# Mixer after a gated recurrence: later loads of U and V, w1 staged in activation buffers, second products in quarters, q and k products on VectorE

## Chip, cores and metric

The kernel runs on one core of one Trainium2 chip. The metric is the device time of one execution in microseconds (us); lower is better. Timed runs and the profiled execution are separate executions of the same program.

## What is computed

```python
f = 1 / (1 + exp(-f_logit))                       # attention, q k v f: (4, 8, 768, 48), float32
for t in range(768):
    state = f[:, :, t, :, None] * state + einsum('bhd,bhe->bhde', k[:, :, t], v[:, :, t])
    y[:, :, t] = einsum('bhd,bhde->bhe', q[:, :, t], state)
x = y.transpose(0, 2, 1, 3).reshape(4, 768, 384)  # then the mixer
u = x + (x.transpose(0, 2, 1) @ U @ V).transpose(0, 2, 1)   # U (768, 32), V (32, 768)
out = u + maximum(u @ w_ch1, 0) @ w_ch2           # w_ch1 (384, 1536), w_ch2 (1536, 384)
```

U, V, w_ch1 and w_ch2 arrive as 64-bit floats, everything else as 32-bit floats.

## The kernel before, in words

The work is cut into 16 **units**: a batch b (0 to 3) and a pair of heads; four units make a batch, and a batch's attention is followed by its **mixer**.

*A unit.* `prepare(n)` has five pieces: `gates` (the sigmoid of f, channels on partitions), `keep` (the scan X over time, L468), `keys` (kT = k times X), `read` (the scan Y, L485, called `read_back` by the loops) and `queries` (qT = q times Y, and the loads of unit n + 2). In batches 0 and 1 the inputs are turned by TensorE (L436) and the products read PSUM on VectorE (L448). In batches 2 and 3 VectorE turns them in blocks of 32 (L417), and the products run on GpSimd (POOL, L451). `attend(n)` has `kept` (kT turned on TensorE and copied to `kb`), `states` (`ds`, then the scan `st`, L560), `scores` (`sc`, masked to A on VectorE), `read` (`y` from the states) and `inner` (`y` from A, then the copy to x). So a unit is a chain that goes back and forth between TensorE, ScalarE and VectorE.

*A mixer.* `low_rank` (x with U), six `mix` (with V, added to x), six `turn`, then for each of three row pairs a: six `ch1` pieces (first product, Relu into the buffer z) and the second product. For batch 0 the second product is six `ch2` pieces, one per row block, each 12 matmuls of 128x128 by 128x384 and one sum on VectorE; a float32 matmul shows as two entries in the profile. For later batches it is the seven-product form `seven`, which needs sums of blocks of w2 (`quarters`) and of z.

*The order.* The orders of TensorE's instructions everywhere, and of VectorE's in batches 0 and 1 and mixer 0, are those of the program text; all other orders are chosen by the scheduler of the framework, which also lets ready transfers pass others. The first loop runs batch 0's units; mixer 0's first products follow without attention beside them; batch 1's units run with `ch2` pieces between their pieces; batches 2 and 3 run with the mixer of the batch before between theirs; mixer 3 is alone at the end. `Fill` spreads the mixer's pieces over 40 slots of a batch, one ahead of each attention piece: every call adds a fortieth of the total cost to what is due, and a piece is issued once half its cost is due. `start_mixer` puts the rest of the old mixer between the opening pieces of the new one.

*Weights.* A load brings 384 64-bit words per partition into `w_raw` (four buffers). `end` makes 32-bit floats: two operations on ScalarE (L62, L63), three on VectorE (L64 to L66), one on POOL (L67). There are 27 loads: U, two halves of V (each row block of V read four times, so that V fills 128 partitions), twelve of w1, twelve of w2. `ahead_by(n, loads)` starts n loads and returns calls, each of which starts the load n places on and converts its own. Loads go through SP's queue (SyncE). The buffers z and zw (three each) hold the Relu's results.

Of the kernel before, what the change touches and what calls it, by code (L numbers as in the profile page):

```python
# [17 lines left out]
WP = 384  # L18
# [13 lines left out]
def weight_loader(nc, pool, dma):  # L32
# [7 lines left out]

    def load(dst, w):
        if w.dtype == F32:
# [8 lines left out]
        def start():  # L51
            raw = T["raw"] = pool.tile([P, WP], U64, name="w_raw", bufs=RAW)[0:rows, 0:n]
            dma.dma_start(out=shaped(raw), in_=w)
# [58 lines left out]
class Mixer:  # L112
# [5 lines left out]
    def __init__(self, tc, b, x, U, V, w1, w2, sums, ident, out, two, three, zp, ps_mm, wide=False):  # L118
# [41 lines left out]
        def ch1(a, j):  # L160

            pm = ps_mm.tile([P, 512], F32, name="pz", tag="mm")
            for i in range(2):
                for m in range(NDC):
                    o = (2 * j + i) * P
                    nc.tensor.matmul(pm[:, i * 2 * P : (i + 1) * 2 * P], lhsT=w1[:, m, o : o + P],  # L166
                                     rhs=uT[a][:, m, :], start=(m == 0), stop=(m == NDC - 1))
            c, k = divmod(2 * j, NI)
            if k == 0:

                own = wide and 2 * a + c >= 3
                z[a, c] = zp.tile([P, NI, 2 * P], F32, name="zw" if own else "z")
            nc.scalar.activation(z[a, c][:, k : k + 2, :].rearrange("p i t -> p (i t)"), pm, AF.Relu)  # L173
# [3 lines left out]

        def ch2(a, s):
            t = 2 * a + s
            pm = ps_mm.tile([P, 512], F32, name="po", tag="mm")  # L180
            for i in range(NFC):
                nc.tensor.matmul(pm[:, 0:DM], lhsT=z[a, i // NI][:, i % NI, s * P : (s + 1) * P],  # L182
                                 rhs=w2[:, i, :], start=(i == 0), stop=(i == NFC - 1))
# [55 lines left out]
        def second(a):  # L239
            if sums is None:  # L240
                return [(2 * NFC * DM, lambda s=s: ch2(a, s)) for s in range(2)]
            return [(2 * NFC * HM * (2 if step < 3 else 1) // 2, lambda step=step: seven(a, step))
                    for step in range(4)]
# [45 lines left out]
def factored_path(ctx, tc, q, k, v, f_logit, moe_U, moe_V, moe_w_ch1, moe_w_ch2, out, ok):  # L289
# [51 lines left out]
    def load_unit(n):  # L341
        b, hp = divmod(n, HP)
        for nm in "fkq":
# [62 lines left out]
    weights += [load(w1[:, :, o : o + P], w1_rows[:, :, o : o + P]) for o in range(0, FF, P)]  # L406
    sums, to_sum = quarters(nc, zp, w2)
# [7 lines left out]
    def turned(t, src_tile):  # L415

        nc.vector.transpose(  # L417
            t.rearrange("p (i c) -> p c i", c=TB),
            src_tile.rearrange("p (c d) -> p c d", d=NB),
        )  # L420
# [3 lines left out]
    def prepare(n):  # L424
# [20 lines left out]
        def operand(nm, of):  # L445
            t = T[nm] = two.tile([P, S], F32, name=f"{nm}T")
            if b < TURNED:
                nc.vector.tensor_tensor(halves(t), on_tensor(nm), halves(T[of]), ALU.mult)  # L448
            else:
                turned(t, r[nm])  # L450
                nc.gpsimd.tensor_tensor(t, t, T[of], ALU.mult)  # L451

# [46 lines left out]
    def attend(n):  # L499
# [9 lines left out]
        def scores():  # L509
# [3 lines left out]
            for c in range(NBL):  # L513
                for par in range(2):
                    for s in range(2):
# [5 lines left out]
                        )  # L521
            nc.vector.tensor_tensor(
                T["A"],
                sc[:, :, 0 : NBL * C].rearrange("p h (c i) -> p h c i", i=C),
                causal.unsqueeze(1).unsqueeze(1).broadcast_to((P, 2, NBL, C)),
                ALU.mult,
            )

# [11 lines left out]
        def states():  # L540

            ds = ps_big.tile([P, 2, 512], F32, name="ds", tag="big")
            for c in range(NBL):
# [15 lines left out]
            st = two.tile([P, D * NCH], F32, name="st")  # L559
            nc.vector.tensor_tensor_scan(  # L560
                st, added[:, 0 : D * NCH], whole.rearrange("p e c -> p (e c)"), 0.0, ALU.add, ALU.mult
            )
            T["st"] = st.rearrange("p (e c) -> p c e", c=NCH)
# [43 lines left out]
    load_unit(1)  # L607
    loads = ahead_by(RAW - 1, weights)
    def attention(b, todo):
# [17 lines left out]
    def start_mixer(b, after):  # L627

        m = mixer(b)
        pieces = after[:1] + m.before[:1] + after[1:2] + m.before[1 : 1 + NBL] + after[2:] + m.before[1 + NBL :]  # L630
        for _, piece in pieces:
            piece()
        return m

    ctx.enter_context(tc.manual_schedule(engines={nc.tensor.engine}))
    with tc.manual_schedule(engines={nc.vector.engine}):
# [4 lines left out]
        for n in range(HP):  # L643
# [362 lines left out]
```

## Time and profile before

| | |
|---|---|
| timed runs | 596.03, 592.49, 591.74 us; median 592.49 |
| profiled execution | 596.04 us, of which the span from the first to the last instruction is 594.2 us |
| mean granted TensorE clock | 0.937 |
| busy: TensorE, VectorE, ScalarE, GpSimd | 528.4, 293.8, 147.2, 63.5 us |
| time per pass: batch 0 / mixer 0's first products / batch 1 / the rest | 0 to 71, 71 to 140, 140 to 252, 252 to 594 us |

In the rows PE is TensorE's matmuls and PEld its weight loads, DVE is VectorE, ACT ScalarE, POOL GpSimd, SPq SyncE's queue. A timeline row gives start, duration, engine, line, instruction, result<-inputs, shapes, count, and in brackets the idle time of the engine before it with what ended that. A row of a group gives busy time and mean nanoseconds of one. A row that begins with a stretch (from:to) gives its length and then the busy time and count of PE, PEld, DVE, ACT and POOL, the granted clock, the DMA engines' busy share and GB/s. The slices are 40 equal parts of the span; a digit is a share in tenths.

### The profile page before, as it was taken

To read this page: it belongs to the slowest core of one execution; us is meant where nothing else is said; L and a number is where in the kernel's file an instruction comes from. 1 tells how busy PE (TensorE), PEld (TensorE's weight loads), DVE (VectorE), ACT (ScalarE), POOL (GpSimd) and SP (SyncE) were. 2 spreads that over 40 slices of the span, in tenths; PEclk is the share of its full clock that TensorE was granted. 3 is DMA by queue.
4 is the path that set the end of the run, shared out by engine and by line. 5 is a ranking of instruction groups with operands and counts; after the bars stand their busy time and mean duration, and the time that the engine had idled before them with its cause. 6 is when DMAs were issued, how large, how long until landed. Compare 5 with 4: busy or idle time off the path is not lost.

```text
span 594.2 us, 11997 instructions
## 1 busy us (share of the span) xinstructions
PE 528.4 (89%) x5277; PEld 437.3 (74%) x5277; DVE 293.8 (49%) x390; ACT 147.2 (25%) x293; POOL 63.5 (11%) x63
## 2 busy tenths in 40 slices
PE   5396886799889869799979997999999999999996
PEld 4286555587667655488968984888989877899996
DVE  4466399910762675749647576047531151122132
ACT  3233256621221210233212221223032102211110
POOL 3001145410000014002021120011200000000000
PEclk9786599999798678999999999999999999999998
DMA  9697447501654532502243343101000000000000
GB/s 151 126 169 130 128 137 206 161 1 20 94 90 68 74 55 54 73 2 41 27 78 45 61 74 41 41 1 22 28 2 2 29 1 29 0 1 28 0 28 32
DMA packets 149077, 34.88 MB, mean 59 GB/s; under 512 B 139544, under 2 KB 147224, under 8 KB 149016
## 3 DMA queue, kind: packets, MB, share of 16 engines
q1 hardware_dynamic: 149016, 34.03, 30.8%
q8 instruction: 43, 0.70, 0.5%
q14 instruction: 18, 0.15, 0.1%
HBM read 29.29 MB, written 4.72 MB: 57 GB/s over the span
## 4 chain that ended last, share of the span: by engine, by line
PE 71%; DVE 18%; DMA 3%; ACT 3%; issue 2%; POOL 2%; SPq 1%; DVEq 0%; POOLq 0%; ACTq 0%
PE pz L166 26%; PE pw L204 19%; PE po L182 9%; PE y L593 5%; DVE w_y L65 3%; DMA f_raw<-in_f_logit_dram 3%; PE y L575 3%; PE pt L436 2%; DVE w_y L66 2%; PE ds L546 2%; DVE st L560 2%; PE pu L147 1%; DVE X L468 1%; DVE fT L417 1%; DVE w_y L64 1%
## 5 line engine op out<-in xcount | busy, mean ns | idle before, releaser
L166 PE MATMUL pz<-uT,w 128*128 128x256 f32 x864 | 194.9, 382 | 11.2 <-ACT z L173 5.4
L166 PEld LDWEIGHTS pz<-uT,w 128*128 128x128 f32 x864 | 161.6, 190 | 37.2 <-issue 5.0
L173 ACT ACTIVATE z<-pz 128x512 f32<-128x512 f32 x63 | 37.5, 595 | 117.6 <-PE pz L166 113.4
L204 PE MATMUL pw<-zw,w_raw 128*128 128x192 f32 x324 | 56.2, 328 | 2.2 <-DVE o L143 2.2
L204 PE MATMUL pw<-w,z 128*128 128x192 f32 x324 | 56.2, 328 | 0.0
L204 PEld LDWEIGHTS pw<-zw,w_raw 128*128 128x128 f32 x324 | 52.8, 190 | 3.7 <-DVE o L143 3.5
L204 PEld LDWEIGHTS pw<-w,z 128*128 128x128 f32 x324 | 52.9, 190 | 1.4 <-DVE x L143 0.5
L143 DVE TENSOR_TENSOR w_raw<-z 128x768 f32<-128x768 f32 x18 | 20.4, 1132 | 57.3 <-ACT z L173 57.2
L451 POOL TENSOR_TENSOR kT<-kT,X 128x768 f32<-128x768 f32 x8 | 14.6, 1821 | 239.1 <-DVE kT L417 239.1
L560 DVE TENSOR_TENSOR_SCAN st<-added,whole 128x576 f32<-128x576 f32 x16 | 21.8, 1363 | 34.5 <-ACT added L552 34.5
L468 DVE TENSOR_TENSOR_SCAN X<-fz,ends 128x768 f32<-128x768 f32 x16 | 28.0, 1753 | 18.4 <-ACT fz L457 7.9
L593 PEld LDWEIGHTS y<-v_nat,A 64*64 64x64 f32 x768 | 30.3, 166 | 7.2 <-ACT seen L582 4.8
L593 PE MATMUL y<-v_nat,A 64*64 64x48 f32 x768 | 32.4, 250 | 3.0 <-ACT seen L582 3.0
L143 DVE TENSOR_TENSOR o<-x,po 128x384 f32<-128x384 f32 x6 | 3.3, 555 | 60.4 <-PE po L182 60.4
L575 PE MATMUL y<-st,qT 48*64 48x48 f32 x704 | 21.2, 275 | 11.3 <-DVE st L560 11.3
L485 DVE TENSOR_TENSOR_SCAN Y<-fz,starts 128x768 f32<-128x768 f32 x16 | 28.0, 1751 | 6.1 <-POOL qT L451 5.9
L575 PEld LDWEIGHTS y<-st,qT 48*64 48x64 f32 x704 | 18.4, 169 | 15.4 <-issue 12.1
L182 PE MATMUL po<-w,z 128*128 128x384 f32 x72 | 28.0, 549 | 0.0
L67 POOL TENSOR_TENSOR w<-w_y,w_r 128x384 int32<-128x384 int32 x24 | 23.9, 996 | 32.4 <-DVE w_y L66 31.0
L182 PE MATMUL po<-w,zw 128*128 128x384 f32 x72 | 25.9, 517 | 0.0
L147 PE MATMUL pu<-h,V 128*128 128x384 f32 x48 | 21.1, 561 | 4.3 <-DVE x L143 3.0
L65 DVE TENSOR_SCALAR w_y<-w_y 128x384 uint32<-128x384 uint32 (+1 forms) x27 | 24.2, 895 | 0.9
(88 smaller groups left out, 561.6 us busy)
## 6 DMA issues: line engine op xcount, KB each, us to landing
w_raw<-in_moe_w_ch_dram SPq DMA_DIRECT2D x24, 384.0 KB, 3.5
v_nat<-in_v_dram SPq DMA_DIRECT2D x32, 144.0 KB, 3.3
out_dram<-o SPq DMA_DIRECT2D x24, 192.0 KB, 1.9
f_raw<-in_f_logit_dram SPq DMA_DIRECT2D x16, 144.0 KB, 4.3
k_raw<-in_k_dram SPq DMA_DIRECT2D x16, 144.0 KB, 4.6
q_raw<-in_q_dram SPq DMA_DIRECT2D x16, 144.0 KB, 4.0
f_raw<-in_f_logit_dram SPq DMA_DIRECT2D x16, 96.0 KB, 3.3
k_raw<-in_k_dram SPq DMA_DIRECT2D x16, 96.0 KB, 2.8
```

The lines of the kernel that those rows point to most:

```text
L65: nc.vector.tensor_scalar(y, y, 3, 0x3FFFFFFF, ALU.logical_shift_left, ALU.bitwise_and)
L67: nc.gpsimd.tensor_tensor(dst.bitcast(I32), shaped(y.bitcast(I32)), shaped(r), ALU.add)
L147: nc.tensor.matmul(pm[:, 0:DM], lhsT=V[:, t * P : (t + 1) * P], rhs=h[0], start=True, stop=True)
L166: nc.tensor.matmul(pm[:, i * 2 * P : (i + 1) * 2 * P], lhsT=w1[:, m, o : o + P], rhs=uT[a][:, m, :], start=(m == 0), stop=(m == NDC - 1))
L173: nc.scalar.activation(z[a, c][:, k : k + 2, :].rearrange("p i t -> p (i t)"), pm, AF.Relu)
L182: nc.tensor.matmul(pm[:, 0:DM], lhsT=z[a, i // NI][:, i % NI, s * P : (s + 1) * P], rhs=w2[:, i, :], start=(i == 0), stop=(i == NFC - 1))
L204: nc.tensor.matmul(pm[:, n * HM : (n + 1) * HM], lhsT=lhs[:, i, :], rhs=rhs[:, i, :], start=(i == 0), stop=(i == NI - 1))
L468: nc.vector.tensor_tensor_scan(backwards(X, S - 1, S), backwards(f, S, S), backwards(ends, S - 1, S), 0.0, ALU.mult, ALU.add,)
L485: nc.vector.tensor_tensor_scan(Y, f[:, 0:S], starts, 0.0, ALU.mult, ALU.add)
L560: nc.vector.tensor_tensor_scan(st, added[:, 0 : D * NCH], whole.rearrange("p e c -> p (e c)"), 0.0, ALU.add, ALU.mult)
L575: nc.tensor.matmul(o(c % 2, par, c // 2), lhsT=T["q"][rows[par], chunk[c]], rhs=T["st"][rows[par], c, :], start=(c <= 2), stop=False, skip ...
L593: nc.tensor.matmul(o(s, par, c), lhsT=T["A"][part[s], par, c, :], rhs=vt[part[s], c, par, :], start=False, stop=True, skip_group_check=True,)
```

## The change

- U, V and the first w1 loads are started after unit 1 instead of ahead of unit 2's loads: nine loads ahead instead of three. U and V are converted after batch 0's last unit. V is read once, into 32 partitions, and copied by three transfers inside SBUF to the other 96.
- The first six w1 loads use the zw buffers as staging, two loads to a buffer. The second half of each z of mixer 0 is now the one in zw.
- In the first loop `read_back` comes ahead of `states` and `scores`.
- `ch2` becomes four pieces of three matmuls; the sum and the store follow the fourth. One such piece follows each piece of `prepare(4)`; eleven go to batch 1's slots; eight stay for `start_mixer(1)`, two on either side of `low_rank`'s end and four after the six `mix`.
- In batches 2 and 3 the rows of q, k and f are loaded in another order, the outputs of VectorE's transpositions are contiguous, and the products with X and Y run on VectorE.
- The mask A and the scan `st` get a higher priority in the scheduler.

```diff
-    def load(dst, w):
+    def load(dst, w, place=None):
...
-            raw = T["raw"] = pool.tile([P, WP], U64, name="w_raw", bufs=RAW)[0:rows, 0:n]
+            raw = pool.tile([P, WP], U64, name="w_raw", bufs=RAW) if place is None else place()
+            raw = T["raw"] = raw[0:rows, 0:n]
...
-                own = wide and 2 * a + c >= 3
+                own = wide and c == 1
...
-        def ch2(a, s):
+        po = {}
+        NQ = 4
+        def ch2(a, s, n):
             t = 2 * a + s
-            pm = ps_mm.tile([P, 512], F32, name="po", tag="mm")
-            for i in range(NFC):
-                nc.tensor.matmul(pm[:, 0:DM], lhsT=z[a, i // NI][:, i % NI, s * P : (s + 1) * P],
+            if n == 0:
+                po[t] = ps_mm.tile([P, 512], F32, name="po", tag="mm")
+            pm = po[t][:, 0:DM]
+            for i in range(n * NFC // NQ, (n + 1) * NFC // NQ):
+                nc.tensor.matmul(pm, lhsT=z[a, i // NI][:, i % NI, s * P : (s + 1) * P],
                                  rhs=w2[:, i, :], start=(i == 0), stop=(i == NFC - 1))
-            o = three.tile([P, DM], F32, name="o")
-            add(o, x[:, t, :], pm[:, 0:DM], ALU.add)
-            store(t, o)
+            if n == NQ - 1:
+                o = three.tile([P, DM], F32, name="o")
+                add(o, x[:, t, :], pm, ALU.add)
+                store(t, o)
...
-                head = src[nm][b, 2 * hp + par].rearrange("(i c) d -> i c d", c=TB)
+                head = src[nm][b, 2 * hp + par].rearrange("(c i) d -> i c d", i=NB)
...
-    weights += [load(V[:, o : o + WP], copies(moe_V, P // R, o, WP)) for o in range(0, S, WP)]
+    weights += [load(V[0:R, o : o + WP], moe_V[:, o : o + WP]) for o in range(0, S, WP)]
...
+    spare = []
+    def place():
+        if not spare:
+            t = zp.tile([P, NFC // 2, 2 * P], F32, name="zw").rearrange("p i t -> p (i t)").bitcast(U64)
+            spare.extend([t[:, 0:WP], t[:, WP : 2 * WP]])
+        return spare.pop(0)
+    FIRST = 6      # w1's load i takes `place` where i < FIRST
...
-            t.rearrange("p (i c) -> p c i", c=TB),
-            src_tile.rearrange("p (c d) -> p c d", d=NB),
+            t.rearrange("p (c i) -> p c i", i=NB), src_tile.rearrange("p (c d) -> p c d", d=NB),
...
-                nc.gpsimd.tensor_tensor(t, t, T[of], ALU.mult)
+                nc.vector.tensor_tensor(t, t, T[of], ALU.mult)
...
+            with tc.high_priority(offset=AHEAD):      # around A's product and around the scan st
...
-    loads = ahead_by(RAW - 1, weights)
...
+        n = len(after) // 4
+        pieces = after[:n] + m.before[:1] + after[n : 2 * n] + m.before[1 : 1 + NBL]
+        pieces += after[2 * n :] + m.before[1 + NBL :]
...
+    early = 1 + S // WP
-            for piece in [kept, keep, keys, states, scores, read_back, gates, read, queries, inner]:
+            for piece in [kept, keep, keys, read_back, states, scores, gates, read, queries, inner]:
                 piece()
-            if n and loads:
-                loads.pop(0)()
+            if n == 1:
+                loads = ahead_by(early + FIRST, weights)
+        for f in loads[:early]:
+            f()
+        loads = loads[early:]
+        for g in range(1, P // R):
+            nc.sync.dma_start(out=V[g * R : (g + 1) * R, :], in_=V[0:R, :])
...
-        todo, after = m.seconds[:4], m.seconds[4:]
-        for i, piece in enumerate(prepare(HP)):
+        n = len(m.seconds) // (NBL // 2)
+        todo, after = m.seconds[:-n], m.seconds[-n:]
+        for piece in prepare(HP):
             piece()
-            if i == 0:
-                todo.pop(0)[1]()
+            todo.pop(0)[1]()
```

More of the change, by code (lines that the diff above doesn't have):

```diff
@@ L240, in second @@
             if sums is None:
-                return [(2 * NFC * DM, lambda s=s: ch2(a, s)) for s in range(2)]
+                return [(2 * NFC * DM // NQ, lambda s=s, n=n: ch2(a, s, n)) for s in range(2) for n in range(NQ)]
             return [(2 * NFC * HM * (2 if step < 3 else 1) // 2, lambda step=step: seven(a, step))
@@ L403, in factored_path @@
     weights = [load(U, moe_U.rearrange("(c p) r -> p c r", p=P))]
-    weights += [load(V[:, o : o + WP], copies(moe_V, P // R, o, WP)) for o in range(0, S, WP)]
+    weights += [load(V[0:R, o : o + WP], moe_V[:, o : o + WP]) for o in range(0, S, WP)]
     w1_rows = moe_w_ch1.rearrange("(c p) f -> p c f", p=P)
-    weights += [load(w1[:, :, o : o + P], w1_rows[:, :, o : o + P]) for o in range(0, FF, P)]
+    spare = []
[5 more added lines that the diff above has]
+    FIRST = 6
+    weights += [
+        load(w1[:, :, i * P : (i + 1) * P], w1_rows[:, :, i * P : (i + 1) * P], place if i < FIRST else None)
+        for i in range(NFC)
+    ]
     sums, to_sum = quarters(nc, zp, w2)
@@ L559, in states @@
             st = two.tile([P, D * NCH], F32, name="st")
-            nc.vector.tensor_tensor_scan(
-                st, added[:, 0 : D * NCH], whole.rearrange("p e c -> p (e c)"), 0.0, ALU.add, ALU.mult
-            )
+            with tc.high_priority(offset=AHEAD):
+                nc.vector.tensor_tensor_scan(
+                    st, added[:, 0 : D * NCH], whole.rearrange("p e c -> p (e c)"), 0.0, ALU.add, ALU.mult
+                )
             T["st"] = st.rearrange("p (e c) -> p c e", c=NCH)
@@ L633, in start_mixer @@
         return m
+    early = 1 + S // WP
+    loads = weights
     ctx.enter_context(tc.manual_schedule(engines={nc.tensor.engine}))
```

13 lines of the change are left out of this document (6 added, 7 removed).

## The prediction

> **What bounds the kernel now.** I read the busy lines first, then the slices.
>
> ```profile
> PE 528.4 (89%) x5277; PEld 437.3 (74%) x5277; DVE 293.8 (49%) x390; ACT 147.2 (25%) x293; POOL 63.5 (11%) x63
> PE   5396886799889869799979997999999999999996
> PEclk9786599999798678999999999999999999999998
> ```
>
> TensorE is the resource: from the 18th slice of 14.85 us (252 us) on it shows 9 but for two slices and the last, at full clock, and nothing in the change removes a matmul. What can be won is its idle time and its low clock, nearly all before 252 us. I split that into four stages and read the waits of each.
>
> **Stage A, the four units of batch 0 (0 to 71 us).**
>
> ```profile
> 13.10 0.81 SPq L53 DMA_DIRECT2D w_raw<-in_moe_U_dram  x1
> 15.48 5.13 SPq L346 DMA_DIRECT2D f_raw<-in_f_logit_dram  x2
> 18.00:23.00 5.00, 0.16 (x12) 0.02 (x4) 3.79 (x3) 1.03 (x3) 0.00 (x0) 0.81 0.44 110
> 23.00:28.00 5.00, 0.00 (x0) 0.00 (x0) 0.00 (x0) 0.98 (x2) 0.00 (x0) 0.50 0.38 102
> 28.55 1.51 PE L436 MATMUL pt<-ident,f_raw 128*128 128x128 f32 x6 [10.39 <-DMA f_raw<-in_f_logit_dram]
> 6.09 1.86 SPq L346 DMA_DIRECT2D f_raw<-in_f_logit_dram  x2
> 11.62 1.51 PE L436 MATMUL pt<-ident,f_raw 128*128 128x128 f32 x6 [1.93 <-DMA f_raw<-in_f_logit_dram]
> 47.78 1.01 PE L546 MATMUL ds<-v_nat,kb 64*64 64x48 f32 x48 [2.85 <-ACT kb L538]
> 60.91 1.36 DVE L560 TENSOR_TENSOR_SCAN st<-added,whole 128x576 f32<-128x576 f32 x1 [4.59 <-ACT added L552]
> 71.25 5.05 PE L147 MATMUL pu<-h,V 128*128 128x384 f32 x8 [0.66 <-ACT h L138]
> ```
>
> U's load and, behind it, V's two stand in the queue ahead of unit 2's f at 15.48. While they drain, TensorE does nothing for 10.39 us and the DMA engines show a busy share of only 0.38 to 0.44: few of them carry V.
>
> **Stage B, the first matmul of mixer 0 (83 to 140 us).** VectorE runs weight conversions back to back:
>
> ```profile
> 89.36 0.35 DVE L64 TENSOR_SCALAR w_y<-w_y 128x384 f32<-128x384 f32 x1
> 89.75 1.05 DVE L65 TENSOR_SCALAR w_y<-w_y 128x384 uint32<-128x384 uint32 x1
> 90.83 0.56 DVE L66 SCALAR_TENSOR_TENSOR w_y<-w_raw,w_y 128x384 uint32<-128x384 uint32 x1
> 119.45 20.99 PE L166 MATMUL pz<-uT,w 128*128 128x256 f32 x96 [0.98 <-ACT zw L173]
> ```
>
> One weight costs 1.95 us (from 89.36 to the next L64 at 91.31); ScalarE fits one Relu between two conversions, so TensorE waits about 1 us per piece, until the conversions end and the last eight pieces (96 entries, 20.99 us) run at 2.6 us each.
>
> **Stage C, batch 1 (140 to 252 us).** Six second-product pieces, `ch2`, of 8 us each stand between small matmuls. VectorE's order is fixed by hand here, and the sum behind a `ch2` waits for its last matmul with everything else behind it:
>
> ```profile
> 140.93 7.91 PE L182 MATMUL po<-w,z 128*128 128x384 f32 x24
> 148.87 0.56 DVE L143 TENSOR_TENSOR o<-x,po 128x384 f32<-128x384 f32 x1 [28.23 <-PE po L182]
> 152.51 0.58 PE L534 MATMUL pt<-ident,kT 64*128 64x64 f32 x12 [1.71 <-DVE kT L448]
> 156.72 10.16 PE L182 MATMUL po<-w,z 128*128 128x384 f32 x24
> 158.00:161.00 3.00, 3.00 (x6) 1.62 (x5) 2.31 (x3) 0.67 (x1) 0.00 (x0) 0.50 0.02 4
> 217.71 1.52 PE L575 MATMUL y<-st,qT 48*64 48x48 f32 x44 [4.37 <-DVE st L560]
> ```
>
> Such gaps are followed by a clock of 0.50, at which the same `ch2` takes 10.16 instead of 7.91 us.
>
> **Stage D, from 252 us.** Two gaps are left, behind the products on POOL:
>
> ```profile
> 299.31 1.76 DVE L468 TENSOR_TENSOR_SCAN X<-fz,ends 128x768 f32<-128x768 f32 x1 [2.01 <-POOL kT L451]
> 360.58 4.17 PE L204 MATMUL pw<-zw,w_raw 128*128 128x192 f32 x24 [2.18 <-DVE o L143]
> 297.00:312.00 15.00, 11.18 (x105) 9.64 (x104) 6.87 (x10) 2.88 (x6) 3.62 (x2) 1.00 0.43 78
> 357.00:372.00 15.00, 11.17 (x55) 7.42 (x56) 9.76 (x17) 1.75 (x4) 0.00 (x0) 1.00 0.31 38
> ```
>
> **The change, part by part.** Each sum is made against the profiled execution, 596.04 us with a span of 594.2; the median of the three timed runs, 592.49, lies 3.55 below it.
>
> *U and V later (stage A).* With U and V out of the way unit 2's f can be issued where U was, at 13.10. Unit 1's f needed 11.62 - 6.09 = 5.5 us from issue to matmul, so unit 2's matmul comes at 18.6 instead of 28.55: 9.9 us won, and some 0.5 us of wait stays. Units 1 and 2 then lose the 2.85 us in which `kb` stood behind a conversion on ScalarE, and pay up to the 1.76 us of a scan (its row stands under stage D): `read_back` now precedes the state scan, and the query product must wait for `read`. I set these two against each other. The state scan of unit 3 goes from 60.91 to 51.0.
>
> Then the price. U and both halves of V are converted behind that unit, on the path:
>
> ```profile
> 44.56 1.89 POOL L67 TENSOR_TENSOR U<-w_y,w_r 128x192 int32<-128x192 int32 x1 [39.30 <-DVE w_y L66]
> 56.47 1.00 POOL L67 TENSOR_TENSOR V<-w_y,w_r 128x384 int32<-128x384 int32 x1 [10.01 <-DVE w_y L66]
> w_raw<-in_moe_w_ch_dram SPq DMA_DIRECT2D x24, 384.0 KB, 3.5
> ...
> out_dram<-o SPq DMA_DIRECT2D x24, 192.0 KB, 1.9
> ```
>
> Scan and mask end at about 53.3. U takes 0.9 on VectorE and 1.89 on POOL; L64 and L65 stretch to a POOL operation's end (1.05 above against 0.35), so each half of V adds its rest of 0.6 to 0.9 and POOL's 1.0: 6.4 us in all, to 59.7. Three copies of V from SBUF to SBUF follow. No row shows one; the store, which lands in 1.9 us, is the nearest: with three issues about 63.2. The queue through which they go is SP's, and ahead of them it holds unit 5's loads and three more w1 loads, two of which wait for a staging buffer that a conversion frees; one such load still under way costs its 3.5 us more and gives the upper end, 67. The lower end is 61.4 (71.25 - 9.9), where the copies cost nothing. I take 64.7, near the store's row: `mix` starts 6.5 us earlier than 71.25, with about 3 us of new wait for V in place of the old 10.
>
> *Staging of w1 in `zw` buffers.* It adds no instruction; six of the twelve loads only start earlier. `zw` is first written by a Relu when j is 3, behind all six conversions. The loads were not late before (VectorE ran without gaps), so 0.
>
> *Stage B.* The same 24 conversions stay at the same pieces: 0. Bounds: -10.7 us if ScalarE's order let every Relu through (18 pieces of 2.6 are 47 of the stage's 57.7 us), and +21 if it put the conversions first (eight more of the pieces left for the end). Nothing in the order of the pieces speaks for either.
>
> *`ch2` in four pieces (stage C).* Now `prepare(4)` alternates with quarters, so X, kT and Y run beside TensorE's quarters, and only one quarter (2 us), not four, lies ahead of a sum. Eleven quarters go out about every 3.6 of the 40 slots. The work of TensorE at full clock:
>
> ```profile
> 148.67 0.82 PE L436 MATMUL pt<-ident,k_raw 128*128 128x128 f32 x6
> 173.58 0.89 PE L516 MATMUL sc<-qT,kT 48*64 48x64 f32 x48
> 176.59 1.23 PE L575 MATMUL y<-st,qT 48*64 48x48 f32 x44 [2.12 <-DVE st L560]
> 168.78 1.60 PE L593 MATMUL y<-v_nat,A 64*64 64x48 f32 x48
> 222.32 0.64 ACT L599 COPY x<-y 128x576 f32<-128x576 f32 x1 [2.90 <-PE y L593]
> ```
>
> A unit has three groups of 0.82 (f, k, q), then 0.58 for `kept`, 1.01 for `ds` (stage A's row), 0.89, 1.23 and 1.60: 7.8 us, four units 31.1. Sixteen quarters are four times 7.91, 31.6. Together 62.7 us, from 140.1 (one group of 0.82 ahead of 140.93) to the copy at 222.3, where 82.2 us were spent: 19.5 is the most to be won. Following the queues piece by piece I find VectorE in time everywhere but in unit 7, whose state scan stands behind unit 8's key transposition and product (about 3 us). That leaves 16.5. In `start_mixer(1)` the next `ch2` meets the full clock too: 10.16 - 7.91 = 2.2 more. For a clock that still dips I take off 1.7. Stage C: 17, between 6 (only the gaps that the rows name: 1.71 + 4.37) and 22.
>
> *Products on VectorE and the new layout.*
>
> ```profile
> L417 DVE STREAM_TRANSPOSE kT<-k_raw 128x768 f32<-128x768 f32 x8 | 16.6, 2071 | 0.0
> L451 POOL TENSOR_TENSOR kT<-kT,X 128x768 f32<-128x768 f32 x8 | 14.6, 1821 | 239.1 <-DVE kT L417 239.1
> L143 DVE TENSOR_TENSOR w_raw<-z,w_raw 128x768 f32<-128x768 f32 x9 | 8.6, 950 | 0.0
> ```
>
> Sixteen products move from 1.82 us on POOL, with a 2 us wait of VectorE behind them, to 0.95 us on VectorE. VectorE is the poorer by 15.2 us of work, but each chain of transposition, product and next scan gets about 1.1 us shorter, twice per unit: I count 2.5 us of the gaps in those two windows, of which 360.58 alone is 2.18. The new order of rows makes the transpositions write contiguously; no row shows such a one: between 0.95 (an ordinary 768-element operation) and 2.07, and I keep 2.07, its own row. The loads for it read rows 32 apart; they have a unit's time of slack. Stage D: 2.5, between 0 and 7.6, the idle time in the two windows above.
>
> The Trainium skill, "SBUF — State Buffer", section "Door 1: The DMA port swizzle", says that an access which leaves a 16-byte line with each element pays a penalty. By that rule the transpositions fall well below 2.07 us (rival 6); whether 2.07 holds such a penalty no row here shows.
>
> **Sum:** 6.5 + 0 + 17 + 2.5 = 26: 570.0 for the profiled execution, 566.5 against the median.
>
> **Rivals.**
> 1. *V takes the place of f.* The copies land at 67 or later, behind the weight loads; the scheduler may also put these ahead of units 2 and 3. For it: SP works in order, and f waited behind V's loads for 5.13 us of issue. Stage A gives 0 to 2: 572.
> 2. *VectorE's fixed order keeps half of stage C,* since the state scans wait for key products and TensorE idles as before. Stage C gives 8: 575.5.
> 3. *Slower: the clock stays at 0.50 in batch 1.* Place: 140 to 222 us. In the rows the clock comes back about 4 us into an 8 us piece (0.50 at 158 to 161, 7.91 us pieces at 1.00); quarters of 2 us never last so long. Then the quarters double (+31.6) and the small groups stretch as `y` does, 1.52 for 1.23 (+7.5): 101.8 against 82.2, 20 lost, 9 won elsewhere: 603.5. It decides if TensorE's gaps between quarters still exceed about 2 us. Against it: after 252 us pieces of 2.6 to 4.2 us (`pz`, `pw`) between the same small groups keep a clock of 0.9 or more in every slice but the last.
> 4. *VectorE as bound in batches 2 and 3:* each product holds back a sum that TensorE waits for, 16 x 0.95 = 15 lost: 584.
> 5. *Stage B's order improves* to its lower bound: 556.
> 6. *A contiguous transposition costs 0.95 us.* Stage D goes to its upper end, 7.6: 561. For it: 2071 against 950 ns for as many elements; against it: the two gaps also hold waits for other engines.
>
> On rival 3, the Trainium skill, "TensorE: Matmul & The Clock Gate", section "Part 1: The HAM clock gate", ties the full clock to a window of some 3.4 us of sustained activity. A stage of 2 us pieces with gaps would not fill it; one without gaps would. The sum without this sentence is the same.
>
> **How the numbers follow.** Forecast 0.45; rivals 1 to 6: 0.15, 0.12, 0.06, 0.06, 0.08, 0.08. Predicted 566.5; the range is 551 (A, C and D at their better ends, or rival 5 and a little) to 583 (rivals 1 and 2 together, nearly rival 4). About 1% is what a measurement of this kernel tells from no change: faster by more 0.89, within 0.05, slower 0.06.
>
> **What would show it.** Right: the f wait near 18 us under 1 us; a wait of `pu` on V of 2 to 4 us; X of unit 4 beside the first quarter; no `po` piece above 2.3 us; no wait of X on POOL. Wrong: slices of clock 0.5 in stage C, `pu` waiting over 6 us, or new waits on VectorE's sums after 252 us.

## The result, and the profile after

| | before | after |
|---|---|---|
| timed runs, median (range) | 592.47 us (591.74 to 596.03) | 558.48 us (557.16 to 559.02) |
| profiled execution, its span | 596.04, 594.2 us | 558.63, 556.8 us |
| mean granted TensorE clock | 0.937 | 0.977 |

The ratio is 0.9409, 95% interval 0.9377 to 0.9441. The forecast was 566.5, in a range of 551 to 583. The page of the changed kernel, its busy line and the slices (13.92 us each):

```profile
PE 511.5 (92%) x5277; PEld 422.3 (76%) x5277; DVE 279.8 (50%) x406; ACT 147.5 (26%) x293; POOL 30.9 (6%) x47
PE   4777577799999899999999999999999999999996
PEclk9997599999999899999999999999999999999999
```

TensorE has the same 5277 entries but 16.9 us less busy time: that much was matmuls at a low clock. From the ninth slice on only one digit before the last is below 9. Marks on the timelines of the profiled executions split the gain by stage:

| us from the span's start | before | after | gain of the stage |
|---|---|---|---|
| f of unit 2 turned | 28.55 | 18.86 | |
| state scan of unit 3 | 60.91 | 47.08 | |
| `mix` starts | 71.25 | 62.35 | A: 8.9 |
| first `pz` of mixer 0, f of unit 4 turned | 82.75, 140.27 | 73.82, 131.34 | B: 0 |
| first `pz` of mixer 1 | 252.18 | 222.08 | C, with `start_mixer`: 21.2 |
| end of the span | 594.2 | 556.8 | D: 7.3 |

The sum is 37.4, all of the difference of the spans. The medians differ by 34.0: the profiled execution of the kernel before was the slowest of its four. Stage A on the changed kernel's timeline:

```profile
18.86 0.85 PE L456 MATMUL pt<-ident,f_raw 128*128 128x128 f32 x6 [1.28 <-DMA f_raw<-in_f_logit_dram]
38.33 3.52 SPq L54 DMA_DIRECT2D zw<-in_moe_w_ch_dram  x6
47.08 1.36 DVE L582 TENSOR_TENSOR_SCAN st<-added,whole 128x576 f32<-128x576 f32 x1 [5.09 <-ACT added L573]
52.16 3.06 SPq L54 DMA_DIRECT2D w_raw<-in_moe_w_ch_dram  x3
53.75 0.99 POOL L68 TENSOR_TENSOR V<-w_y,w_r 32x384 int32<-32x384 int32 x1 [0.94 <-DVE w_y L67]
55.31 2.20 SPq L684 DMA_DIRECT2D V<-V  x3
62.35 6.87 PE L148 MATMUL pu<-h,V 128*128 128x384 f32 x12 [6.03 <-DMA V<-V]
```

The wait for f fell from 10.39 to 1.28 us. A new wait of 6.03 us stands in front of `mix`, for the three copies of V. They were issued behind three w1 loads, and landed 5.3 to 6.0 us after their issue.

Stage C as one stretch, from unit 4's f to mixer 1's first `pz`, of the kernel before and of the changed one (length, then busy time of PE, PEld, DVE, ACT and POOL, clock, DMA share, GB/s):

```profile
140.27:252.18 111.91, 97.60 (x1059) 65.67 (x1058) 64.69 (x71) 22.82 (x50) 8.42 (x4) 0.86 0.45 70
```

```profile
131.34:222.08 90.74, 87.15 (x1060) 56.86 (x1058) 62.22 (x77) 22.79 (x49) 0.00 (x0) 0.98 0.46 78
```

Of the 21.2 us, 10.5 are busy time at a low clock (97.60 to 87.15) and 10.7 idle time (14.3 to 3.6). Stage D, two groups of the changed kernel, and the whole stage of the kernel before and of the changed one:

```profile
L438 DVE STREAM_TRANSPOSE kT<-k_raw 128x768 f32<-128x768 f32 x8 | 7.7, 966 | 0.0
L471 DVE TENSOR_TENSOR kT<-kT,X 128x768 f32<-128x768 f32 x8 | 7.6, 953 | 0.2
```

```profile
252.18:594.20 342.02, 327.17 (x3089) 288.60 (x3089) 146.64 (x194) 69.31 (x132) 22.80 (x12) 1.00 0.14 27
222.08:556.80 334.72, 326.94 (x3091) 288.60 (x3089) 134.69 (x204) 69.58 (x132) 0.00 (x0) 1.00 0.16 29
```

A contiguous transposition takes 966 ns, not 2071. TensorE's busy time in the stage is the same within 0.3 us; its idle time fell from 14.9 to 7.8 us, and that is the gain.

### The profile page after: what moved, and what is told of

Read it like the earlier page. It is cut to its first block, busy times and chain, and to the rows that moved or that the text cites. A ratio compares the mean times of both kernels' runs of the same rounds, so it can differ in the third digit from the quotient of the medians.

```text
span 556.8 us, 11971 instructions
## 1 busy us (share of the span) xinstructions
PE 511.5 (92%) x5277; PEld 422.3 (76%) x5277; DVE 279.8 (50%) x406; ACT 147.5 (26%) x293; POOL 30.9 (6%) x47
## 4 chain that ended last, share of the span: by engine, by line
PE 77%; DVE 13%; SPq 3%; DMA 2%; ACT 2%; issue 1%; POOL 0%; ACTq 0%; DVEq 0%; POOLq 0%
PE pz L167 30%; PE pw L212 23%; PE po L189 7%; PE y L615 4%; DVE w_y L66 4%; PE y L597 3%; PE pt L456 2%; PE ds L567 2%; DVE w_y L67 2%; PE pu L148 2%; PE sc L536 2%; SPq L364 1%; DVE X L488 1%; DVE st L582 1%; DVE w_y L65 1%
## 5 line engine op out<-in xcount | busy, mean ns | idle before, releaser
L174 ACT ACTIVATE z<-pz 128x512 f32<-128x512 f32 x63 | 37.4, 594 | 118.9 <-PE pz L167 114.8
L144 DVE TENSOR_TENSOR w_raw<-z 128x768 f32<-128x768 f32 x18 | 17.1, 951 | 58.6 <-ACT z L174 58.6
L615 PEld LDWEIGHTS y<-v_nat,A 64*64 64x64 f32 x768 | 25.8, 145 | 5.4 <-issue 4.5
L615 PE MATMUL y<-v_nat,A 64*64 64x48 f32 x768 | 27.8, 229 | 0.5 <-ACT seen L604 0.5
L597 PE MATMUL y<-st,qT 48*64 48x48 f32 x704 | 19.8, 263 | 6.6 <-DVE st L582 6.6
L189 PE MATMUL po<-w,z 128*128 128x384 f32 x72 | 25.3, 495 | 0.0
L597 PEld LDWEIGHTS y<-st,qT 48*64 48x64 f32 x704 | 16.9, 147 | 10.8 <-issue 8.4
L66 DVE TENSOR_SCALAR w_y<-w_y 128x384 uint32<-128x384 uint32 (+2 forms) x27 | 24.4, 904 | 0.9
L148 PEld LDWEIGHTS pu<-h,V 128*128 128x128 f32 x48 | 9.0, 210 | 19.5 <-issue 8.5
L144 DVE TENSOR_TENSOR w_y<-x,pw 128x192 f32<-128x192 f32 x9 | 3.2, 354 | 39.4 <-ACT w_y L225 39.4
```

The lines of the kernel that those rows point to most:

```text
L66: nc.vector.tensor_scalar(y, y, 3, 0x3FFFFFFF, ALU.logical_shift_left, ALU.bitwise_and)
L148: nc.tensor.matmul(pm[:, 0:DM], lhsT=V[:, t * P : (t + 1) * P], rhs=h[0], start=True, stop=True)
L189: nc.tensor.matmul(pm, lhsT=z[a, i // NI][:, i % NI, s * P : (s + 1) * P], rhs=w2[:, i, :], start=(i == 0), stop=(i == NFC - 1))
L597: nc.tensor.matmul(o(c % 2, par, c // 2), lhsT=T["q"][rows[par], chunk[c]], rhs=T["st"][rows[par], c, :], start=(c <= 2), stop=False, skip ...
L615: nc.tensor.matmul(o(s, par, c), lhsT=T["A"][part[s], par, c, :], rhs=vt[part[s], c, par, :], start=False, stop=True, skip_group_check=True,)
```

## Experiments

All runs in one view: the ratio to the kernel before on the same chip, and from the profiled execution the start of `mix`, the length of stage C (f of unit 4 to mixer 1's first `pz`) and the rest behind it (D). Where a text below gives a difference to the changed kernel in us, it is the difference of the ratios times 592.5. The last three columns come from one execution each: the start of `mix` lies between 60.36 and 62.87 in the seven runs that leave stage A as changed (the changed kernel, c1 to c4, d1, d2), so less than 2.5 us there says nothing.

| run | median us | ratio (95%) | mix | C | D |
|---|---|---|---|---|---|
| before | 592.47 | 1 | 71.25 | 111.91 | 342.0 |
| changed | 558.48 | 0.9409 (0.9377 to 0.9441) | 62.35 | 90.74 | 334.7 |
| c1_whole | 574.13 | 0.9668 (0.9638 to 0.9698) | 61.88 | 107.16 | 334.7 |
| c2_sum_later | 571.19 | 0.9620 (0.9583 to 0.9657) | 61.30 | 103.93 | 334.8 |
| c4_before_read | 566.25 | 0.9553 (0.9530 to 0.9577) | 60.45 | 98.17 | 334.6 |
| c3_packed | 563.23 | 0.9500 (0.9469 to 0.9530) | 62.87 | 94.29 | 334.6 |
| d2_old_rows | 564.28 | 0.9500 (0.9470 to 0.9531) | 62.84 | 92.93 | 338.4 |
| d1_pool | 557.79 | 0.9402 (0.9379 to 0.9424) | 60.36 | 90.31 | 335.7 |
| a1_old_order | 557.16 | 0.9382 (0.9358 to 0.9406) | 61.87 | 89.08 | 334.7 |
| a2_V_direct | 552.22 | 0.9286 (0.9261 to 0.9311) | 60.62 | 91.05 | 334.7 |
| a3_before_V_split | 590.54 | 0.9927 (0.9900 to 0.9955) | 66.62 | 111.92 | 341.8 |
| a4_copies_first | 553.94 | 0.9335 (0.9317 to 0.9353) | 58.33 | 89.09 | 334.9 |
| e1_no_stage_prio | 553.34 | 0.9342 (0.9318 to 0.9365) | 59.51 | 89.08 | 334.8 |
| b2_best | 551.44 | 0.9299 (0.9270 to 0.9328) | 58.54 | 89.36 | 334.7 |

### Stage C: the pieces of ch2

**c1_whole** undoes the quarters.

```diff
-        NQ = 4
+        NQ = 1
...
+        todo, after = m.seconds[:4], m.seconds[4:]      # prepare(4) and start_mixer as before the change
```

> The changed kernel with each second product of mixer 0 in one piece again, placed as before the change (four in the fill, the first behind the f transposes of unit 4, two in the next mixer's start); all else as changed. If VectorE's hand-made order, with a sum behind 8 us of matmuls, was what stage C lost, all of the stage returns: about +21 us, 579, with a clock slice of 0.5 to 0.7 in 130 to 220 us and a wait of over 20 us of a sum on po. If the stage gained through something else (the earlier loads, the high clock carried over from stage A), less than half returns: 568 or below.

It lost 15.3 us, and its stage C is 16.4 us longer. So the quarters carry most of the stage's 21.2, not all: 4.8 of the difference to the kernel before come from elsewhere. Unit 5 on its timeline, and behind it stretches with the clock (the last figure but two):

```profile
164.42 1.52 PE L597 MATMUL y<-st,qT 48*64 48x48 f32 x44 [2.13 <-DVE st L582]
167.34 2.80 PE L615 MATMUL y<-v_nat,A 64*64 64x48 f32 x48
170.07 6.25 PE L189 MATMUL po<-w,z 128*128 128x384 f32 x12
```

```profile
168.00:170.00 2.00, 2.00 (x41) 1.98 (x38) 0.40 (x1) 0.00 (x0) 0.00 (x0) 0.50 0.60 82
172.00:174.00 2.00, 2.00 (x4) 1.01 (x3) 0.00 (x0) 0.00 (x0) 0.00 (x0) 0.50 0.84 156
174.00:176.00 2.00, 2.00 (x7) 1.26 (x6) 0.00 (x0) 0.00 (x0) 0.00 (x0) 0.91 0.00 0
```

The wait is for the state scan, and no `ch2` stands near it. A wait of 2.13 us is followed by some 10 us at half clock, in which half a `ch2` takes 6.25 instead of 4.03 us.

**c2_sum_later** keeps the whole pieces and moves only the sum and the store.

```diff
+            def end():
                 o = three.tile([P, DM], F32, name="o")
                 add(o, x[:, t, :], pm, ALU.add)
                 store(t, o)
+            ends[t] = end           # a piece of cost 0, later in the fill
```

> As the run with whole second products, but sum and store of each are a piece of their own, of cost 0, which comes some slots later in the fill (for the first one: behind the five pieces of unit 4's preparation); TensorE's pieces are still 8 us long. If it is the place of the sum in VectorE's order that stops TensorE, most of the 21 us stays won: 560 to 566, and X of unit 4 runs beside the first second product. If the length of the piece on TensorE itself is what costs (the small matmuls of the units come in too late for the engines behind them), it stays near the run with whole pieces: 575 to 580.

Only 2.8 of c1's 15.3 us came back, and the two intervals overlap. The first X of unit 4 did what the theory said, in c1 and then in c2:

```profile
139.47 0.55 DVE L144 TENSOR_TENSOR o<-x,po 128x384 f32<-128x384 f32 x1 [28.23 <-PE po L189]
139.94 1.75 DVE L488 TENSOR_TENSOR_SCAN X<-fz,ends 128x768 f32<-128x768 f32 x1
```

```profile
131.98 1.76 DVE L491 TENSOR_TENSOR_SCAN X<-fz,ends 128x768 f32<-128x768 f32 x1 [21.33 <-ACT fz L480]
163.03 1.24 PE L600 MATMUL y<-st,qT 48*64 48x48 f32 x44 [2.50 <-DVE st L585]
182.14 1.52 PE L600 MATMUL y<-st,qT 48*64 48x48 f32 x44 [2.12 <-DVE st L585]
```

X moved 8 us forward. But `y` of the later units waits for `st` as before. In unit 5 it is 2.50 us; there the moved sum, 0.55 us, now stands between X and kT, without a wait of its own. In unit 6 it is 2.12 us with no sum ahead of `st`. The theory that a sum holds VectorE back falls, but for its first place.

A second theory, formed from these two runs: in each unit TensorE has nothing of its own between `scores` and `read`, while the state scan goes through ScalarE and VectorE. Eleven quarters reach nearly every such place; three whole pieces reach one.

**c4_before_read** puts that to the test: whole pieces with their sums behind them, placed by hand.

```diff
-                fill()
+                if b > 1:
+                    fill()
+                elif piece is read and n > HP:      # units 5, 6 and 7 of batch 1
+                    fill.pieces.pop(0)[1]()
```

> The run with whole second products again (574.1), but the three pieces in the fill of batch 1 are put by hand directly ahead of read (the matmuls that wait for the state scan) of units 5, 6 and 7. There y waited 2.1, 2.1 and 3.0 us for st, each time with a low clock behind it. If the pieces' number and places, not their length, lost the stage, these three waits and the low clock behind them go and only unit 4's wait comes: 562 to 567. If a piece of 8 us is itself the cause (VectorE waits behind its sum, the next small group comes late), it stays at 571 to 577.

It came out in the range of the second theory. The `y` of unit 4, which has no piece ahead of it, and of unit 5:

```profile
147.31 1.52 PE L597 MATMUL y<-st,qT 48*64 48x48 f32 x44 [3.36 <-DVE st L582]
165.50 1.23 PE L597 MATMUL y<-st,qT 48*64 48x48 f32 x44
```

No wait for `st` is left in units 5 to 7; stage C is 9.0 us shorter than c1's, by placing alone, with pieces of 8 us, and the whole kernel 6.8 us faster than c1. (The 9.0 comes from a profiled execution 3.7 us below c4's median; the 6.8 is the safer figure.) Of the 7.4 us of stage C that still divide c4 from the changed kernel, 5.1 are more idle time of TensorE: unit 4 keeps its waits, 1.71 us for kT and 3.36 for `st`.

**c3_packed** keeps the quarters but puts the first four together.

```diff
-        for piece in prepare(HP):
-            piece()
-            todo.pop(0)[1]()
+        for i, piece in enumerate(prepare(HP)):
+            piece()
+            for _ in range(4 if i == 0 else 0):
+                todo.pop(0)[1]()
```

> The changed kernel (quarters), but the first four quarters stand together behind the f transposes of unit 4, as the whole piece did before, and the other pieces of unit 4's preparation follow without quarters between them. Under the theory of VectorE's order only X, the key product and Y of unit 4 come late, behind one sum: +3 to +6 us, 562 to 565, with the wait on kT of unit 4 back (1.71 us before) and a low clock for a few us behind it. If the alternation with the preparation is what won the stage, +15 or more: 574.

It lost 5.4 us by the medians; in the profiled execution stage C is 3.6 us longer. The wait on kT did not come back: a quarter of the fill now stood in front of it, and from unit 4's f to its kT TensorE had no gap at all. The edit also leaves twelve quarters to the fill instead of eleven, which moves all of them, and none stands directly ahead of a `y` that waits for `st` any more. Two of the four units, each `y` with the quarter behind it:

```profile
165.05 1.24 PE L597 MATMUL y<-st,qT 48*64 48x48 f32 x44 [1.59 <-DVE st L582]
166.22 3.87 PE L189 MATMUL po<-w,z 128*128 128x384 f32 x6
181.45 1.24 PE L597 MATMUL y<-st,qT 48*64 48x48 f32 x44 [1.59 <-DVE st L582]
182.62 2.20 PE L189 MATMUL po<-w,z 128*128 128x384 f32 x6
```

All four wait for `st` (2.07 us in unit 4, 1.59 in the others), where the changed kernel has one such wait. So what c3 lost in stage C fits the second theory again; a price of its own for the missing alternation is not seen.

### Stage D: transposition and products

**d2_old_rows** and **d1_pool** undo one half each.

```diff
-                head = src[nm][b, 2 * hp + par].rearrange("(c i) d -> i c d", i=NB)
+                head = src[nm][b, 2 * hp + par].rearrange("(i c) d -> i c d", c=TB)      # d2, and the output's stride
...
-                nc.vector.tensor_tensor(t, t, T[of], ALU.mult)
+                nc.gpsimd.tensor_tensor(t, t, T[of], ALU.mult)                            # d1
```

> The changed kernel with the old order of rows in batches 2 and 3, so that the transpositions write with a stride again (2.07 us each); the k and q products stay on VectorE. If the contiguous transposition carries stage D, most of its 7.5 us goes: +5 to +8, 564 to 566, and a gap is back near 297 to 312 or 357 to 372 us. If the move of the products to VectorE carries it, +0 to +2: 558 to 561.

> The changed kernel with the k and q products of batches 2 and 3 back on POOL; the contiguous transposition stays. With the old rows and VectorE's products 5.8 us of stage D were lost. If the transposition alone carries the stage, +0 to +2: 558.5 to 560.5. If both are needed, since POOL's product of 1.8 us is in the same chain, +4 to +7: 562.5 to 565.5, with waits on a product of POOL near 297 to 312 or 357 to 372 us.

The transposition's group in d2, then in d1 with the scan that follows a product:

```profile
L438 DVE STREAM_TRANSPOSE kT<-k_raw 128x768 f32<-128x768 f32 x8 | 16.6, 2074 | 0.0
```

```profile
L438 DVE STREAM_TRANSPOSE kT<-k_raw 128x768 f32<-128x768 f32 x8 | 7.7, 965 | 0.0
L505 DVE TENSOR_TENSOR_SCAN Y<-fz,starts 128x768 f32<-128x768 f32 x16 | 28.0, 1750 | 7.6 <-POOL qT L471 7.5
```

With before and after this fills a square for stage D: strided with POOL 342.0, strided with VectorE 338.4, contiguous with POOL 335.7, contiguous with VectorE 334.7. Alone the products give 3.6 and the transposition 6.3; together 7.3, since they shorten the same chain. So d2 loses 3.7 us here, not all of the stage. In d1 VectorE waits for POOL again (7.5 us ahead of Y), and TensorE hardly notices: stage D is 1.0 us longer, the whole time the same within the intervals. The transposition also gave some 2 us of stage C (92.93 against 90.74; 89.08 to 91.05 in the runs with the same pieces), where unit 8's keys are made during unit 7: there `y` waits 2.29 us in d2, 1.58 in the changed kernel.

### Stage A: loads, order and copies

**a3_before_V_split** is the kernel before with V's load in another form.

```diff
-    weights += [load(V[:, o : o + WP], copies(moe_V, P // R, o, WP)) for o in range(0, S, WP)]
+    weights += [load(V[:, o : o + WP], [moe_V[:, o : o + WP]] * (P // R)) for o in range(0, S, WP)]
...              # start(): one dma_start for each part of 32 partitions
```

> The kernel before, with each half of V loaded by four loads of 32 partitions instead of one load with an outermost dimension of 4; place in the queue and bytes as before. If the form of V's load is what held unit 2's f back (10.39 us of waiting at a DMA share of 0.38 to 0.44), the wait falls under 4 us, the DMA share rises to 0.8 or more and the time falls by 5 to 8 us, to 585 to 588. If its place in the queue and its bytes are what counts, the wait stays above 8 us and the time at 592 to 594.

Its timeline at unit 2's f, and the two stretches around it:

```profile
23.94 1.51 PE L441 MATMUL pt<-ident,f_raw 128*128 128x128 f32 x6 [5.43 <-DMA f_raw<-in_f_logit_dram]
```

```profile
18.00:23.00 5.00, 0.52 (x20) 0.33 (x13) 3.87 (x3) 2.17 (x5) 0.00 (x0) 1.00 0.88 184
23.00:28.00 5.00, 4.06 (x56) 3.64 (x56) 0.00 (x0) 1.03 (x3) 0.00 (x0) 1.00 0.99 170
```

Between the two theories: the DMA share rose from 0.38 to 0.44 up to 0.88 and 0.99, and the wait for f fell by 5.0, to 5.43 us. So about half of it was V's form and half its place. The whole kernel gained 0.7%. The Trainium skill, "DMA: Bandwidth & Descriptors", section "Why a DMA increments its semaphore by 16 and not by 1", says that a transfer uses the largest number of engines up to 16 that divides the outermost sizes of both sides; that would be 4 for V's old load and 16 for each of the new ones. The shares point the same way; they count all transfers of the stretch, so the number of engines itself is not shown here.

**a1_old_order** puts `states` and `scores` ahead of `read_back` again.

```diff
-            for piece in [kept, keep, keys, read_back, states, scores, gates, read, queries, inner]:
+            for piece in [kept, keep, keys, states, scores, read_back, gates, read, queries, inner]:
```

> The changed kernel with the old order in the first units: states and scores ahead of read_back. The state scan of unit 3 came 13.8 us earlier with the change, 3.9 more than the missing wait for f explains. If the new order won these 3.9 us, they go: about +4, 562, with the state scan of unit 3 near 51. If they came from the higher clock and from ScalarE without conversions, it stays within 1 us: 558 to 559.5, with the scan near 47.

The state scan of unit 3:

```profile
47.80 1.36 DVE L582 TENSOR_TENSOR_SCAN st<-added,whole 128x576 f32<-128x576 f32 x1 [5.85 <-ACT added L573]
```

The scan came at 47.80 and the time did not rise: the intervals of both kernels overlap. The new order is worth nothing that can be measured here.

**a4_copies_first** issues the copies ahead of the three w1 loads, and **a2_V_direct** has none: each half of V is loaded as in a3.

```diff
-        for f in loads[:early]:
-            f()
-        loads = loads[early:]
+        for _, end in weights[:early]:
+            end()
...              # the three copies V<-V
+        for start, _ in weights[early + FIRST : 2 * early + FIRST]:
+            start()
+        loads = loads[early:]
```

> The changed kernel with V's three copies from SBUF to SBUF issued ahead of the three weight loads that stand before them in SP's queue (the sixth to eighth block of w1). In the changed kernel the copies land 5.3 to 6.0 us after their issue and mix waits 6.03 us. If they wait for SP and the weight loads, mix starts near 57.5 and the time falls by 4 to 5, to 554, with a wait for V under 1 us. If a copy from SBUF to SBUF is slow by itself, they still land after more than 5 us; only the 3 us of issue ahead of them are won: 556 to 557.5.

> The changed kernel with each half of V loaded into all four groups of 32 partitions by four loads, and without the copies from SBUF to SBUF. In the changed kernel mix waits 6.03 us for these copies. If that wait is on the path, the mix starts near 57.5 instead of 62.35 and the time falls by about 5, to 553.5. If stage B, whose pace the weight conversions set, gives it back (the first w1 conversions come no earlier), under 1.5 us stays: 557 to 559.

Rows of a4, then of a2:

```profile
54.47 1.87 SPq L683 DMA_DIRECT2D V<-V  x3
58.33 3.15 PE L148 MATMUL pu<-h,V 128*128 128x384 f32 x8 [2.00 <-DMA V<-V]
```

```profile
60.62 7.04 PE L153 MATMUL pu<-h,V 128*128 128x384 f32 x12 [0.66 <-ACT h L144]
72.32 15.78 PE L172 MATMUL pz<-uT,w 128*128 128x256 f32 x72 [0.38 <-ACT uT L164]
```

In a4 the copies land 2.4 us after their issue (median), not 5.4. `mix` starts 4.0 earlier, at the higher clock (8 matmul entries in 3.15 us), and the kernel gains 4.4. That it was the loads in front of the copies shows in all the runs that have copies: the sooner these follow the last of the three loads, the later they land.

| run | issue of the copies, us behind the loads' | landing, median us | wait of `mix` for V |
|---|---|---|---|
| changed | 0.1 | 5.4 | 6.03 |
| a1 | 0.4 | 4.8 | 4.39 |
| c1 | 0.8 | 4.5 | 4.06 |
| c2, d2 | 1.1 | 4.0 | 3.48, 3.90 |
| c4 | 1.2 | 3.2 | 2.59 |
| d1 | 1.3 | 3.0 | 2.56 |
| c3 | 2.6 | 2.5 | 2.10 |
| e1 | 2.7 | 2.1 | 1.63 |
| a4 | none ahead | 2.4 | 2.00 |

So the 6.03 us of the profiled execution is the longest wait of all; the same stage in c1 to c4, d1 and d2 waits 2.10 to 4.06.

In a2 the wait for V is gone and the kernel gains 7.3. Its profiled execution ran stage A at a lower clock (0.66 to 0.91 between 16 and 40 us, where the changed kernel has 1.00), so `mix` starts only at 60.62; 3.4 us of its gain lie in stage B, where six pieces of `pz` (72 entries, 15.78 us) run without a wait instead of three: 54.15 us against 57.52. ScalarE's order there came out otherwise; why is not settled.

**e1_no_stage_prio** leaves out the staging in `zw` and the priorities.

```diff
-    FIRST = 6
+    FIRST = 0
...              # and both "with tc.high_priority" lines removed
```

> The changed kernel without two of its parts: no weight is staged in the zw buffers (three loads ahead, as before the change), and mask product and state scan have no priority on VectorE. If both are worth nothing, as the prediction put the staging, it stays within 2 us: 557 to 560.5. If the early loads carry part of the gain in stages A and B, the first weight conversions come late and 3 to 8 us are lost: 561.5 to 566.

Neither: it is 4.0 us faster than the changed kernel.

SP's queue and the start of `mix`:

```profile
45.13 8.09 SPq L54 DMA_DIRECT2D w_raw<-in_moe_w_ch_dram  x3
55.88 1.87 SPq L682 DMA_DIRECT2D V<-V  x3
59.51 3.15 PE L148 MATMUL pu<-h,V 128*128 128x384 f32 x8 [1.63 <-DMA V<-V]
```

With six loads fewer on the way the three loads ahead of the copies are issued earlier, the copies land in 2.1 us, and `mix` starts at 59.51. The conversions lose nothing: stage B is 57.51. The two parts were left out together, so that it is the staging is argued, from the copies; the priorities were not tried by themselves. a4, which keeps both and only puts the copies first, is as fast as e1 (0.9335 and 0.9342): without loads in front of the copies, no cost of either part is left to be seen.

### Stage B: the Relu

**b2_best** is a2 with the Relu put ahead.

```diff
+            with tc.high_priority(offset=AHEAD):
-            nc.scalar.activation(z[a, c][:, k : k + 2, :].rearrange("p i t -> p (i t)"), pm, AF.Relu)
+                nc.scalar.activation(z[a, c][:, k : k + 2, :].rearrange("p i t -> p (i t)"), pm, AF.Relu)
```

> The changed kernel with V loaded directly into the four groups (552.2 in its run) and with the Relu behind each first product of mixer 0 put ahead in ScalarE's order. In stage B TensorE waits about 1 us for a Relu per piece while weights are converted (8.8 us in eight named waits in the changed kernel, 4.9 in five with V loaded directly). If ScalarE's order makes these waits, they go: -5 to -10 us against 552, to 542 to 547. If VectorE's conversions set the pace through something else (the weights themselves come late), nothing changes or weights come late in place of Relus: 551 to 556.

ScalarE's timeline in stage B, without the second operation of each conversion:

```profile
88.83 0.56 ACT L68 ACTIVATE w_y<-w_raw 128x384 f32<-128x384 f32 x1 [0.93 <-POOL w L73]
...
89.74 0.57 ACT L180 ACTIVATE z<-pz 128x512 f32<-128x512 f32 x1
90.78 0.56 ACT L68 ACTIVATE w_y<-w_raw 128x384 f32<-128x384 f32 x1 [0.47 <-POOL w L73]
...
92.73 0.57 ACT L68 ACTIVATE w_y<-w_raw 128x384 f32<-128x384 f32 x1 [0.94 <-POOL w L73]
```

Stage B is 54.14 us, as in a2. ScalarE still has one Relu to two conversions: the priority did not change the order, so whether another order would win the 5 us of waits stays open. a2 and b2, alike within their intervals, are the fastest versions tried: both intervals lie below the changed kernel's.

## Why the prediction was right, and where it was not

Direction and range held. The gain was 34.0 us by the medians where 26 was forecast: three of the four stages were sized too small, and one cause was wrong. Of the signs named, X of unit 4 ran beside the first quarter and no X waited for POOL. But f waited 1.28 us instead of under 1, one quarter took 3.86 us where 2.3 was the limit, and `pu` waited 6.03 us, just over the 6 that were to speak against the forecast.

**Stage A, 6.5 forecast, 8.9 measured: two misses that partly cancelled.** The first step held (9.9 us for f; 28.55 to 18.86 is 9.7). The next one set the relief of `kb` (2.85) against a price of the new order (1.76). a1 shows that the order has no price, and the scan of unit 3 came at 47.08 instead of 51.0. U's addition on POOL took 0.59 us where I kept the one row of 1.89, and the conversions ended at 54.74, not 59.7. The copies I priced with the store's 1.9 us; they took 5.4, and the wait was 6.03 where I had written 2 to 4. That is rival 1's mechanism, loads ahead of the copies in SP's queue, within the forecast's own case; the 6.03 is also partly chance, since five of the other six executions with this stage A lie in 2 to 4. `mix` then ran at half clock and took 11.47 us to the first `pz`, against 10.12 in a4. That is no loss, for the kernel before took 11.50, but a gain that was left behind.

**Staging, 0 forecast: it very likely cost time.** e1, without it and without the priorities, was 4.0 us faster. I looked only at whether the loads were late before; I did not ask what else would come later with 2.3 MB (six of 384 KB) more on the way. Rival 1 named the queue and I gave it 0.15.

**Stage B, 0 forecast, 0 measured** (57.52 both times). That it has room below shows in a2's 54.15.

**Stage C, 17 forecast, 21.2 measured: the size was near, the cause partly wrong.** "The sum behind a `ch2` waits for its last matmul with everything else behind it" is worth 2.8 us by the medians, with intervals that overlap (c1 to c2). What counts is how many of the idle places between small matmuls get a piece, and that each wait there also cost clock. From c1 to the changed kernel TensorE's idle time in the stage fell by 9.0 and its busy time by 7.5 us. The account by matmul work (82.2 spent, 62.7 needed) did not need the cause, which is why the number held. Two terms were mis-sized: unit 7's wait was 1.58, not 3 (2.29 with the old transposition, in d2), and `start_mixer` gained 3.5 us, from unit 7's last `y` to the first `pz` (29.9 to 26.4), more than the 2.2 of one piece.

**Stage D, 2.5 forecast, 7.3 measured.** I kept 2.07 us for the transposition; it took 0.966. Rival 6 had this, with 7.6 for the stage. The Trainium skill, "SBUF — State Buffer", section "Door 1: The DMA port swizzle", gave the ground for it, a penalty for leaving a 16-byte line with each element; 2074 against 966 ns in two kernels that differ in the row order alone agrees, and the page has no figure. The products by themselves gave 3.6 (d2), near my 2.5.

**Rival 3, slower by clock, did not come.** Stage C's clock is 0.98, and the quarters leave TensorE only 3.6 us of idle time there; gaps were the point from which I had it decide.

## What to carry to other kernels

Cut filler work to the size and number of the idle places it is to fill, and put a piece directly ahead of each wait: whole pieces in the right three places won back 6.8 us, a moved sum 2.8, which the noise nearly covers. An early load is not free even if its buffer is: what is issued soon after it through the same queue lands later (5.4 us instead of 2.1 to 2.5 here), so start it when it is needed and put the small transfer that someone waits for in front. Price a short wait of TensorE with the half-clock stretch behind it, and look at the outermost dimension of a load before moving it.

## What the runs showed of the hardware that I had not expected

The same wait did or did not cost the clock. In unit 7 of the changed kernel `y` waits 1.58 us for `st`, and the next quarter runs at half clock:

```profile
189.12 1.24 PE L597 MATMUL y<-st,qT 48*64 48x48 f32 x44 [1.58 <-DVE st L582]
190.29 3.86 PE L189 MATMUL po<-w,zw 128*128 128x384 f32 x6
```

In a4, e1 and a1 the same instruction waits 1.58, 1.59 and 1.59 us and the six microseconds behind it run at 1.00 (a4's row):

```profile
183.72:189.72 6.00, 6.00 (x102) 4.35 (x103) 6.00 (x6) 2.32 (x6) 0.00 (x0) 1.00 0.00 0
```

That is 1.65 us of stage C (90.74 against 89.09). In d1 a wait of 1.60 us was followed by a quarter of 3.90 us. In c3 (rows above) it happened within one execution: three waits of 1.59 us, of which one was followed by a quarter of 3.87 us and two by quarters of 2.20. The Trainium skill, "TensorE: Matmul & The Clock Gate", section "Part 1: The HAM clock gate", says that the window of activity runs freely and does not start with the work; a wait near the limit would then trip it or not by its phase. These runs agree with that; none sets the phase.

A transposition of 128x768 in blocks of 32 took 2.07 us with a strided output and 0.966 with a contiguous one. Three copies from SBUF to SBUF of 96 KB each landed in 2.1 us (median, e1) to 5.4 us (the changed kernel), the later the sooner they followed three loads of 384 KB in the same queue.
